# Value products in the order of head pairs 0, 2, 1, 3, and the seven-product first layer one step earlier

## The chip, the cores and the metric

The kernel runs on one core of a Trainium2 chip. A core has five engines that run side by side, each through its own queue of instructions in order: TensorE (PE, matmuls, with a weight load PEld for each), VectorE (DVE), ScalarE (ACT), GpSimd (POOL) and SyncE (SP), which here issues DMA transfers. They wait for each other through semaphores. The metric is the device time of one execution in microseconds; a profile is one execution taken by the hardware profiler, and its span runs from its first instruction to its last.

## The reference

Attention with pooled keys and values, followed by a two-layer MLP. There are 8 batches, 8 heads, 576 tokens and head size 64; the MLP has 512 inputs, 2048 hidden units and 512 outputs.

```
k_p = mean of k over 8 successive tokens            # 72 pooled keys for each head
v_p = mean of v over 8 successive tokens            # 72 pooled values
scores = q @ k_p.T / sqrt(64)
attn = exp(scores - max) / sum
x = attn @ v_p, heads side by side                  # 4608 tokens x 512
h = x @ w_in
out = gelu_tanh(h) @ w_out
```

## The kernel before, in words

The 4608 tokens go through in nine groups of 512: groups 0 to 7 are the first 512 tokens of a batch, and group R (number 8) collects the last 64 tokens of all eight batches. They run in the order 0 to 6, R, 7. Group 0 has its own opening. Every later group is a pass of the loop at the end of the kernel, counted by `n_`; "step n" below is the pass with `n_ == n`, so step 1 does the MLP of group 1, step 2 that of group 2, step 3 that of group 3.

A step does the two MLP layers of its group on TensorE and, between those matmuls, the attention of the next group, so that the next step finds its x ready. The work is not placed by a scheduler: the order on each engine is the order in which the kernel's text issues it. `at(hooks, s, f, ...)` hangs a function on a slot s, and the MLP calls the slot before its matmuls: slots 0 to 63 belong to the first layer, slots 64 to 175 to the second (112 matmuls of 128x256, one slot each). A function that is hung on a slot issues its instructions there, on whichever engine it uses, and each engine then takes them in that order.

The first layer comes in two forms. The plain form (`hidden_two`, then `hidden` for the other columns) makes 64 matmuls of 128x512. The fast form (`hidden_fast`) computes half of the layer with seven products in place of eight, in Strassen's manner: 56 matmuls of 128x256 (`product`, L465), 32 plain ones of 128x512 (L374), and on VectorE the differences of x that it needs (`x_sums`, L449) and the sums of the products (L493, L501, L504, L508), with copies on ScalarE. Between its first and second product it calls `rest()`, which is `values(g, 1)`: the second half of its own group's value products. Which form a step takes is decided by `fast = n_ >= 3`.

The second layer has seven products in every step: they run in the order 1, 2, 6, 5, 7, 3, 4 (L577), of 16 matmuls each. Four of the inputs are sums of activations made on VectorE by `g_sums` (L425 to L429). Products 1, 6, 7 and 4 accumulate one after another in the same PSUM tile `xs`; between them it is copied out by ScalarE (`x_copy`, L92), or added out by VectorE (`x_add`, L562), and the next product on it waits for that.

The attention of the next group, by the functions that the change touches:

- `load_kv` issues the loads of K and V on SP (L112 for the large parts, L107 and L105 for two half blocks); `load_q` those of q (L121).
- `pool` sums eight rows in three VectorE instructions (L149, L151, L152); its first is stage 0 and the other two are stage 1. Blocks 0 to 4 hold K and the first V rows, blocks 5 to 8 the rest of V.
- `dup_k`, `kT_tile` and `k_transpose_dma` (L165, L207) transpose the pooled keys by DMA, and `k_spread` copies them into the block form `kbd` (L92 or L94).
- `spread_v` multiplies the pooled values by a mask into the block form `vbd`, on POOL (L172); `spread_gated` is the same behind a small instruction that makes POOL wait.
- `cast_gated` casts q on POOL (L94), and `q_transpose_dma` transposes it on SP (L228).
- `scores` (L244), `exps` (ScalarE, L253), `sums` and `norm` (VectorE, L260, L269, L275; the second of the four on POOL), and `e_transpose_dma` (SP, L302) make the normalised weights, 128 tokens at a time. The buffers of `exps` are three for four parts.
- `values` (L337) multiplies the weights with `vbd`, 256 tokens at a time. For groups 1 to 7 a call makes 16 matmuls: eight with 32 rows (`SMALL`), then eight with 64 rows (`BIG`), and in each of the two passes two matmuls for each of four head pairs. A matmul uses one 32x64 or 64x64 tile of the array, given by the row where its weights start and by which half of the output's partitions it writes:

```
    BIG = [(64, 0), (0, 1), (64, 1), (0, 2), (0, 3), (64, 3), (0, 4), (64, 4)]
    SMALL = [(0, 1), (64, 1), (0, 2), (64, 2), (96, 2), (32, 3), (96, 3), (32, 4)]
                for pr in range(HP):
                    for hh in range(2):
                        r0, c = part[2 * pr + hh]
```

In this list head pairs 0 and 1 use the same two tiles, and so do pairs 2 and 3. The result is cast to bf16 by ScalarE and VectorE (L92, L94), and the first layer reads it.

Of the kernel before, what the change touches and what calls it, by code (L numbers as in the profile page):

```python
# [19 lines left out]
def kernel(  # L20
# [21 lines left out]
    nc = tc.nc  # L42
    B, H, S, D = q.shape
# [6 lines left out]
    HP = H // 2  # L50
# [39 lines left out]
    def copy(eng, out, in_):  # L90
        if eng is nc.scalar:
            eng.copy(out=out, in_=in_)  # L92
        else:
            eng.tensor_copy(out=out, in_=in_)  # L94
# [227 lines left out]
    def values(g, half, split=True):  # L322

        eT, t0 = st[g]["eT"], 256 * half
        if half == 0 or not split:
            xo = psum.tile([128, HP, 256], F32, name="xo", tag="sc", bufs=2)
            dst = [xo[:, pr, :] for pr in range(HP)]
        else:
            xo = [psum.tile([128, 2, 256], F32, name="xo", tag="mm", bufs=4) for _ in range(2)]
            dst = [xo[pr // 2][:, pr % 2, :] for pr in range(HP)]  # L330
        if g < B:
            for part, rows_ in ((SMALL, 32), (BIG, 64)):
                for pr in range(HP):
                    for hh in range(2):
                        r0, c = part[2 * pr + hh]
                        n = dict(PARTS[pr])[c]
                        nc.tensor.matmul(out=dst[pr][64 * hh:64 * hh + 64],  # L337
                                         lhsT=vbd[r0:r0 + rows_, g, n, 64 * hh:64 * hh + 64],
                                         rhs=eT[r0:r0 + rows_, 2 * half:2 * half + 2, c, :],
                                         start=(part is SMALL and pr % 2 == 0), stop=(part is BIG), skip_group_check=True)  # L340
        else:
            for pr in range(HP):
                for b in range(4):
                    p0 = 64 * (b % 2)
                    for x, (c, n) in enumerate(PARTS[pr]):
                        nc.tensor.matmul(out=dst[pr][:, 64 * b:64 * b + 64], lhsT=vbd[:, 4 * half + b, n, :],  # L346
                                         rhs=eT[:, 2 * half + b // 2, c, p0:p0 + 64], start=(x == 0), stop=(x == 1))
        xT = st[g]["xT"]
        if half == 0 or not split:
            copy([nc.scalar, nc.vector][half], xT[:, :, t0:t0 + 256], xo)  # L350
        else:
            for i, eng in enumerate((nc.scalar, nc.vector)):
                copy(eng, xT[:, 2 * i:2 * i + 2, t0:t0 + 256], xo[i])
# [408 lines left out]
    def at(hooks, s, f, *a):  # L762
        hooks.setdefault(s, []).append(lambda: f(*a))

    def tail_of_attention(hooks, n, va):
        at(hooks, va, xT_tile, n)
        at(hooks, va, nc.scalar.preload_act_table_set, GELU_SET)
        at(hooks, va, values, n, 0)
        at(hooks, va, values, n, 1, False)

    hooks = {}
# [46 lines left out]
    for n_, g in enumerate(seq):  # L818
        if n_ == 0:
            continue  # L820
        hooks = {}
        fast = n_ >= 3
        if n_ == 1:
            for i in range(1, 4):
                at(hooks, i, w_sums, i, 0, NP, nc.vector)
            at(hooks, 36, g_sums, 0, 4)
            at(hooks, 57, g_sums, 4, 6)
        elif fast:
            at(hooks, 41, g_sums, 0, 2, (0,))
            at(hooks, 57, g_sums, 2, 6, (0,))  # L830
            at(hooks, 65, g_sums, 6, 8, (0,))
            at(hooks, 65, g_sums, 0, 8, (1,))
        else:
            at(hooks, 20, g_sums, 0, 2)
            at(hooks, 36, g_sums, 2, 4)
            at(hooks, 57, g_sums, 4, 6)
        if not fast:
            at(hooks, 65, g_sums, 6, 8)
        if n_ + 1 < len(seq):
            n = seq[n_ + 1]  # L840
            b = B - 1 if n == R else n
            kv = n != B - 1
            if n_ == 1:
                for j in range(4):
                    at(hooks, 28 + 4 * j, cast_q, n, j, j + 1, nc.scalar)
                at(hooks, 41, qT_tile, n)
                at(hooks, 41, q_transpose_dma, n)
            if kv and not fast:
                t0 = 22 if n_ == 1 else 12
                at(hooks, t0, pool, b, 0, 5)  # L850
                at(hooks, t0, dup_k, b, 0, 5)
                at(hooks, t0, kT_tile, b, None)
                at(hooks, t0, k_transpose_dma, b)
                t1 = t0 + (16 if n_ == 1 else 24)
                at(hooks, t1, pool, b, 5, 9)
                at(hooks, t1, spread_v, b, nc.gpsimd)
                at(hooks, 56, k_spread, b, [nc.vector, nc.vector])
            elif kv:
                at(hooks, 17, pool, b, 0, 5, (1,))
                at(hooks, 17, dup_k, b, 0, 5)  # L860
                at(hooks, 17, kT_tile, b, None)
                at(hooks, 17, k_transpose_dma, b)
                at(hooks, 17, spread_gated, b)
                at(hooks, 40, k_spread, b, [nc.gpsimd, nc.gpsimd])
            if fast:
                at(hooks, 2, qT_tile, n)
                at(hooks, 2, q_transpose_dma, n)
                sc_at = [76, 76, 100, 100]
                norm_at = [84, 88, 106, 106]
            else:  # L870
                sc_at = [68, 68, 94, 94]
                norm_at = [81, 97, 104, 114]
            for j in range(4):
                at(hooks, sc_at[j], scores, n, j)
                at(hooks, max(sc_at[j], 80), exps, n, j)
            at(hooks, norm_at[0], eT_tile, n)
            if fast:
                for j in (2, 3):
                    at(hooks, norm_at[j], sums, n, j)
            for j in range(4):  # L880
                at(hooks, norm_at[j], norm, n, j, nc.gpsimd if j == 1 else nc.vector)
                at(hooks, norm_at[j], e_transpose_dma, n, j)
            at(hooks, 64 + 66, nc.scalar.preload_act_table_set, GELU_SET)
            at(hooks, 64 + 100, xT_tile, n)
            at(hooks, 64 + 100, values, n, 0)
            if n_ < 2:
                at(hooks, 64 + 107, values, n, 1)
        if n_ + 2 < len(seq):
            n2 = seq[n_ + 2]
            s2 = 44 if n_ == 1 else 8 if n2 == R else 57  # L890
            at(hooks, s2, q_tile, n2)
            if n2 == R:
                at(hooks, s2, load_q, n2, 0, 2, nc.sync)
                at(hooks, 30, load_q, n2, 2, 4, nc.sync)
            else:
                at(hooks, s2, load_q, n2, 0, 4, nc.sync)
            at(hooks, 64 + 52, cast_gated, n2)
            if n_ < 2:
                at(hooks, 64 + 100, qT_tile, n2)
                at(hooks, 64 + 100, q_transpose_dma, n2)  # L900
                at(hooks, 64 + 100, load_kv, n2, (1,))
            elif n2 != B - 1:
                b2 = B - 1 if n2 == R else n2
                at(hooks, 64 + 84, pool, b2, 5, 9, (0,))
                at(hooks, 64 + 97, pool, b2, 5, 9, (1,))
                at(hooks, 64 + 98, pool, b2, 0, 5, (0,))
            if n_ == 1:
                at(hooks, 45, load_kv, n2, (0,))
            else:
                at(hooks, 28, load_kv, n2)  # L910
        mlp(g, hooks, n_ + 1 == len(seq), fast, lambda: values(g, 1))
# [30 lines left out]
```

## Time and profile before

| what | us |
|---|---|
| median of 3 runs (280.68 to 280.84) | 280.75 |
| the profiled execution | 280.68 |
| its span | 278.8 |
| PE busy in it | 271.8 |
| DVE busy | 224.3 |
| ACT busy | 176.3 |
| POOL busy | 64.7 |
| value products of groups 1 to 7 (L337), one call of 16 matmuls | 0.70 |

A row of a timeline gives the start in us from the beginning of the span, the length in us, the engine, the line, the operation, what it writes and reads, the shapes and the count; in brackets stands how long the engine was idle before it and what ended that. The chain that ended last gives start, length and what ran. A row of a table by stretch gives the stretch, its length, then the busy time and the count of PE, PEld, DVE, ACT and POOL, then the granted clock, the DMA share and GB/s.

### The profile page before, as it was taken

The page shows a single profiled execution, that of the slowest core. Times are in us where ns is not written, and L with a number is a line of the kernel's source. Part 1 is how long each engine was busy: PE and PEld are TensorE (multiplying, and loading weights), DVE is VectorE, ACT ScalarE, POOL GpSimd, SP SyncE. Part 2 cuts the span into 40 slices and gives each one's busy share as a digit, 9 for nine tenths or more (in the row PEclk, how much of TensorE's full clock was granted, in tenths as well). Part 3 has the DMA queues.
Part 4 walks back from the last instruction along what each step waited for, and adds up shares of the span by engine and source line. Part 5 has one row for each costly group of instructions (what it writes and reads, how often), then busy time and mean ns, then how long its engine had stood idle before and what let it go on. Part 6 is the DMA issues. An engine that isn't in the chain of part 4 may idle for free.

```text
span 278.8 us, 6535 instructions
## 1 busy us (share of the span) xinstructions
PE 271.8 (97%) x2686; PEld 191.8 (69%) x2686; DVE 224.3 (80%) x370; ACT 176.3 (63%) x258; POOL 64.7 (23%) x103
## 2 busy tenths in 40 slices
PE   8989999999999999999999999999999999999995
PEld 3668844445864587668766876687668966876684
DVE  5886869999966989989898989898989378937832
ACT  1586575487637764796479647964796469647820
POOL 4640162003130314221422142214221300100000
PEclk9999999999999999999999999999999999999999
DMA  7999999998989895998579969996941550263013
GB/s 227 310 195 296 372 386 212 312 334 204 264 186 250 275 261 150 168 281 235 161 161 267 251 162 209 224 239 168 159 150 27 160 137 2 26 141 83 1 40 113
DMA packets 71695, 54.36 MB, mean 195 GB/s; under 512 B 45554, under 2 KB 57842, under 8 KB 71666
## 3 DMA queue, kind: packets, MB, share of 16 engines
q1 hardware_dynamic: 69410, 51.72, 72.7%
q0 software_dynamic: 2112, 2.10, 4.7%
q8 instruction: 21, 0.34, 0.5%
q10 hardware_dynamic: 144, 0.13, 0.1%
q14 instruction: 8, 0.07, 0.1%
HBM read 36.70 MB, written 9.44 MB: 165 GB/s over the span
## 4 chain that ended last, share of the span: by engine, by line
PE 87%; DVE 7%; DMA 4%; SPq 1%; issue 0%; POOL 0%
PE mm L577 33%; PE mm L374 22%; PE c L465 13%; PE mm L385 5%; PE xo L337 3%; PE x L577 3%; PE sc L244 2%; DMA q_sb<-in_q_dram 2%; DMA qT<-q_b 2%; DVE den L260 1%; PE mm L522 1%; DVE eb L275 1%; PE mm L390 1%; DVE kv L149 1%; DVE eb L287 1%; PE xo L346 1%
## 5 line engine op out<-in xcount | busy, mean ns | idle before, releaser
L374 PE MATMUL mm<-xT,w_in_b 128*128 128x512 bf16 x304 | 69.9, 379 | 0.0
L577 PEld LDWEIGHTS <-gT 128*128 128x128 bf16 x512 | 48.7, 98 | 8.9 <-issue 1.4
L376 ACT ACTIVATE gT<-mm 128x512 bf16<-128x512 f32 x76 | 43.9, 598 | 15.3 <-PE mm L374 14.9
L374 PEld LDWEIGHTS <-w_in_b 128*128 128x128 bf16 x304 | 29.7, 98 | 30.7
L577 PEld LDWEIGHTS <-stage 128*128 128x128 bf16 x384 | 37.2, 98 | 4.5
L92 ACT CAST xT<-xo 128x512 bf16<-128x512 f32 (+1 forms) x17 | 13.4, 786 | 31.1 <-PE xo L337 26.2
L172 POOL TENSOR_TENSOR vbd<-kvb,vmask 128x256 bf16<-128x256 bf16 (+2 forms) x40 | 22.2, 578 | 36.4 <-DVE kvb L152 27.4
L577 PE MATMUL mm<-tw,gT 128*128 128x256 bf16 x240 | 30.0, 273 | 0.0
L260 DVE TENSOR_REDUCE den<-e 128x8 f32<-128x576 f32 x36 | 26.1, 738 | 4.4 <-ACT e L253 4.4
L577 PE MATMUL mm<-w_out_b,gT 128*128 128x256 bf16 x240 | 29.1, 273 | 0.0
L92 ACT COPY osb<-mm 128x512 f32<-128x512 f32 x30 | 17.6, 585 | 18.0 <-PE mm L577 16.8
L577 PE MATMUL mm<-tw,stage 128*128 128x256 bf16 x224 | 27.6, 273 | 0.0
L253 ACT ACTIVATE e<-sc 128x576 f32<-128x576 f32 x36 | 22.5, 654 | 6.5 <-PE sc L244 3.9
L275 POOL TENSOR_TENSOR eb<-e,r 128x576 bf16<-128x576 f32 x7 | 8.0, 1149 | 72.3 <-DVE r L269 66.1
L94 POOL CAST q_b<-q_sb 128x1024 bf16<-128x1024 f32 (+1 forms) x15 | 19.3, 1307 | 19.1 <-DMA q_sb<-in_q_dram 19.1
L149 DVE TENSOR_TENSOR kv<-kv 128x1024 f32<-128x1024 f32 (+3 forms) x19 | 21.0, 1106 | 3.3 <-DMA kv<-in_k_dram 2.2
L465 PEld LDWEIGHTS <-ws 128*128 128x128 bf16 x192 | 18.8, 98 | 6.0
L275 DVE TENSOR_TENSOR eb<-e,r 128x576 bf16<-128x576 f32 x25 | 20.0, 799 | 0.9
L94 DVE CAST xT<-xo 128x512 bf16<-128x512 f32 (+1 forms) x10 | 7.5, 745 | 13.5 <-PE xo L337 8.3
L465 PE MATMUL c<-tt,ws 128*128 128x256 bf16 x144 | 17.7, 273 | 0.0
L425 DVE TENSOR_TENSOR stage<-gT 128x512 bf16<-128x512 bf16 (+1 forms) x25 | 13.1, 526 | 3.4 <-ACT gT L481 1.9
L385 PE MATMUL mm<-xT,w_in_b 128*128 128x256 bf16 x128 | 15.6, 273 | 0.1
(105 smaller groups left out, 413.5 us busy)
## 6 DMA issues: line engine op xcount, KB each, us to landing
kv<-in_k_dram SPq DMA_DIRECT2D x7, 1024.0 KB, 6.7
q_sb<-in_q_dram SPq DMA_DIRECT2D x7, 1024.0 KB, 9.6
kv<-in_v_dram SPq DMA_DIRECT2D x6, 1024.0 KB, 8.2
out_dram<-osb SPq DMA_DIRECT2D x12, 512.0 KB, 3.2
out_dram<-osb SPq DMA_DIRECT2D x11, 256.0 KB, 3.3
kv<-in_v_dram SPq DMA_DIRECT2D x4, 512.0 KB, 10.1
w_in_b<-in_moe_w_in_dram POOLq DMA_DIRECT2D x4, 512.0 KB, 6.7
w_out_s<-in_moe_w_out_dram SPq DMA_DIRECT2D x2, 1024.0 KB, 13.4
```

What stands on the lines that cost most here:

```text
L92: eng.copy(out=out, in_=in_)
L94: eng.tensor_copy(out=out, in_=in_)
L149: add(out=t[:, :, 0:4, :], in0=t[:, :, 0:4, :], in1=t[:, :, 4:8, :], op=ALU.add)
L172: eng.tensor_tensor(out=vbd[p0:128, b, n0:n1, :].rearrange("p (c r) (hh d) -> p c (r hh) d", c=max(m, 1), d=D), in0=kvb[p0:128, 4 + c0:4 + ...
L253: nc.scalar.activation(out=e.rearrange("p (x h) s -> p x (h s)", x=2), in_=sc[:, :, 0:4 * Sp], func=ACT.Exp, scale=1.0 / 64.0)
L260: nc.vector.reduce_sum(out=den, in_=e, axis=AX.X)
L275: eng.tensor_tensor(out=o.rearrange("p (pr hh s) -> p hh pr s", hh=2, s=Sp), in0=e.rearrange("p (hh pr) s -> p hh pr s", hh=2), in1=r.rear ...
L374: nc.tensor.matmul(out=hp, lhsT=w_in_b[:, ko, fo * 128:(fo + 1) * 128], rhs=st[g]["xT"][:, ko, :], start=(i == 0), stop=(i == KO - 1))
L376: nc.scalar.activation(out=gT[:, fo, :], in_=hp, func=ACT.Gelu_apprx_tanh)
L385: nc.tensor.matmul(out=hp[:, f, :], lhsT=w_in_b[:, ko, (fo + f) * 128:(fo + f + 1) * 128], rhs=st[g]["xT"][:, ko, c0:c0 + 256], start=(ko ...
L465: nc.tensor.matmul(out=acc[:, m, :], lhsT=lhs(i, m), rhs=rhs(i), start=bool(fresh and i == 0 and m % 2 == 0), stop=(i == 1), skip_group_ch ...
L577: nc.tensor.matmul(out=xs[p] if acc is xs else acc[:, p, :], lhsT=lt, rhs=rt, start=bool(fresh and m == 0 and (p == 0 or (last and acc is ...
```

## The change

The value products of groups 1 to 7 go through the head pairs in the order 0, 2, 1, 3, so that four successive matmuls are given four different tiles of the array.

Step 2 takes the fast form of the first layer (`fast = n_ >= 2`). With it, the second half of group 2's value products is made by `rest()` inside step 2, no longer at slot 171 of step 1. The rest of step 2's schedule becomes that of the fast steps: the sums of activations at their slots, the scores at 76 and 100, the norms at 84 to 106, `k_spread` on POOL at slot 40, the transposes of q at slot 2 (it was slot 164 of step 1). The first pooling stage of group 3's K runs at slot 162 of step 1, and its second stage at slot 17 of step 2. The load of group 3's V moves from slot 164 of step 1 to slot 3 of step 2, behind the transpose of q. Its pooling, all three instructions, and its spread stand at slot 41 of step 2 (in steps 3 and later, the pooling of V is done at slots 148 and 161 of the step before, and the spread at slot 17).

```diff
--- before.py
+++ after.py
@@ -330,7 +330,7 @@
             for part, rows_ in ((SMALL, 32), (BIG, 64)):
-                for pr in range(HP):
+                for pr in (0, 2, 1, 3):
                     for hh in range(2):
@@ -819,7 +819,7 @@
-        fast = n_ >= 3
+        fast = n_ >= 2
@@ -860,11 +860,17 @@
                 at(hooks, 17, k_transpose_dma, b)
-                at(hooks, 17, spread_gated, b)
+                if n_ == 2:
+                    at(hooks, 41, pool, b, 5, 9)
+                    at(hooks, 41, spread_v, b, nc.gpsimd)
+                else:
+                    at(hooks, 17, spread_gated, b)
                 at(hooks, 40, k_spread, b, [nc.gpsimd, nc.gpsimd])
             if fast:
                 at(hooks, 2, qT_tile, n)
                 at(hooks, 2, q_transpose_dma, n)
+                if n_ == 2:
+                    at(hooks, 3, load_kv, n, (1,))
                 sc_at = [76, 76, 100, 100]
                 norm_at = [84, 88, 106, 106]
@@ -883,8 +889,6 @@
             at(hooks, 64 + 100, values, n, 0)
-            if n_ < 2:
-                at(hooks, 64 + 107, values, n, 1)
@@ -895,14 +899,11 @@
             at(hooks, 64 + 52, cast_gated, n2)
-            if n_ < 2:
-                at(hooks, 64 + 100, qT_tile, n2)
-                at(hooks, 64 + 100, q_transpose_dma, n2)
-                at(hooks, 64 + 100, load_kv, n2, (1,))
-            elif n2 != B - 1:
+            if n2 != B - 1:
                 b2 = B - 1 if n2 == R else n2
-                at(hooks, 64 + 84, pool, b2, 5, 9, (0,))
-                at(hooks, 64 + 97, pool, b2, 5, 9, (1,))
+                if n_ >= 2:
+                    at(hooks, 64 + 84, pool, b2, 5, 9, (0,))
+                    at(hooks, 64 + 97, pool, b2, 5, 9, (1,))
                 at(hooks, 64 + 98, pool, b2, 0, 5, (0,))
```

## The prediction

> **What bounds the kernel now.** I read the page's busy times and the chain that ended last, then the same chain in order of time, then busy times per step, then single instructions of VectorE and TensorE.
>
> ```profile
> PE 271.8 (97%) x2686; PEld 191.8 (69%) x2686; DVE 224.3 (80%) x370; ACT 176.3 (63%) x258; POOL 64.7 (23%) x103
> PE 87%; DVE 7%; DMA 4%; SPq 1%; issue 0%; POOL 0%
> ```
>
> TensorE sets the end, but VectorE's 80% is an average. In order of time, the first value products of steps 1, 2 and 3 and the scores of step 2 stand in the chain like this:
>
> ```profile
> 78.77 0.70 PE xo L337 x16
> ...
> 96.10 0.38 PE sc L244 x32
> ...
> 99.43 0.57 PE sc L244 x32
> ...
> 107.75 0.70 PE xo L337 x16
> ...
> 135.58 0.70 PE xo L337 x16
> ```
>
> So step 2, which has the plain first product, takes 107.75 - 78.77 = 28.98 us, and step 3, which has the seven-product form, 27.83 us. Busy times in these two stretches:
>
> ```profile
> 78.77:107.75 28.98, 28.97 (x276) 18.25 (x280) 22.67 (x42) 18.34 (x28) 6.27 (x10) 1.00 0.99 240
> 107.75:135.58 27.83, 27.83 (x300) 20.49 (x304) 25.59 (x42) 19.04 (x26) 8.12 (x13) 1.00 0.81 208
> ```
>
> TensorE (first pair after the length) is never idle in either. VectorE (third) has 2.2 us free in step 3: this is what the change must live on. Step 3 is my template: the changed step 2 has its instructions, with one block more on VectorE. A time t of step 3 is t - 28.98 in step 2. VectorE's rows of step 3 around that place, and the TensorE product that waits for the last of them:
>
> ```profile
> 121.51 0.43 DVE L427 TENSOR_TENSOR stage<-gT 128x512 bf16<-128x512 bf16 x1
> 122.27 0.69 DVE L425 TENSOR_TENSOR stage<-gT 128x1024 bf16<-128x1024 bf16 x1 [0.33 <-ACT gT L481]
> 127.18 0.75 DVE L260 TENSOR_REDUCE den<-e 128x8 f32<-128x576 f32 x1 [0.19 <-ACT e L253]
> 133.50 0.69 DVE L562 TENSOR_TENSOR osb<-mm,osb 128x512 f32<-128x512 f32 x1
> 134.98 0.60 PE L577 MATMUL mm<-tw,gT 128*128 128x256 bf16 x4
> ```
>
> From 121.94 to 134.19 VectorE pauses only 0.33 and 0.19 us. L562 reads the PSUM pieces xs, into which product 4 accumulates next, from 134.98: the margin is 134.98 - 134.19 = 0.79 us.
>
> **The fast form itself.** Removed are 64 matmuls of 128x512 (1.89 + 12.09 = 13.98 us in the chain); added are 56 of 128x256 and 32 of 128x512, which in step 3 take 0.87 + 0.98 + 1.73 + 1.75 + 0.86 + 0.87 + 0.86 + 1.75 + 3.45 = 13.12. The second scores go from 0.57 to 0.38, since they come later than the exponentials that free their PSUM. With small shifts the whole is the difference of the steps: -1.15 us. The form's sums and copies on VectorE and ScalarE are in the template.
>
> **The block that step 3 does not have.** Group 3's value rows are pooled wholly at hook 41 of step 2 (three VectorE instructions), just after the 121.51 row, where step 3 has none. Their price, and what POOL does meanwhile, stand in steps 1 and 2:
>
> ```profile
> 90.69 1.22 DVE L149 TENSOR_TENSOR kv<-kv 128x1024 f32<-128x1024 f32 x1
> 91.94 0.69 DVE L151 TENSOR_TENSOR kv<-kv 128x512 f32<-128x512 f32 x1
> 92.67 0.43 DVE L152 TENSOR_TENSOR kvb<-kv 128x256 bf16<-128x256 f32 x1
> 93.01 0.93 DVE L94 COPY kbd<-kTd 64x288 bf16<-64x288 bf16 x2
> ...
> 65.35 1.90 POOL L172 TENSOR_TENSOR vbd<-kvb,vmask 128x256 bf16<-128x256 bf16 x3
> 65.52 0.73 DVE L425 TENSOR_TENSOR stage<-gT 128x512 bf16<-128x512 bf16 x1
> 66.35 0.65 DVE L426 TENSOR_TENSOR gT<-gT 128x512 bf16<-128x512 bf16 x1
> 67.91 0.42 DVE L425 TENSOR_TENSOR stage<-gT 128x512 bf16<-128x512 bf16 x1
> 68.44 0.42 DVE L426 TENSOR_TENSOR gT<-gT 128x512 bf16<-128x512 bf16 x1
> ```
>
> The three take 93.01 - 90.69 = 2.32 us, start to start. They release POOL's four spreads (2.47 us in steps 1 and 2), which then run beside the next VectorE sums of gT, L425 and L426, at 128x1024. Beside spreads these sums were slower at 128x512: 0.73 against 0.42 and 0.65 against 0.42, factors 1.74 and 1.55. On 0.69 each that is 0.51 + 0.38 = 0.9 us. Bounds: nothing, if the longer form doesn't suffer (L149 took 1.22 at 134.11 beside POOL's casts and 1.22 at 90.69 with POOL idle), and the spreads' own 2.47 if it were held off altogether. I take 0.9, from the same instructions.
>
> So VectorE is later at L562 by 2.32 - 0.33 - 0.19 + 0.9 = 2.70 us, and product 4 starts 2.70 - 0.79 = 1.91 us late: +1.91. Two earlier waits lie inside this. Product 7 must wait for ScalarE's copy of xs (L92, 129.94 in step 3), queued behind the fourth exponential, which waits for VectorE's first norm to free its buffer. Product 6 needs the last L427 (125.73, so 128.6 now) for its seventh matmul at about 128.7. Transposes of eb are late too, but TensorE is then as late; the last landed 0.57 us before use in step 3 (138.00 against 138.57), so up to 0.3 may be added.
>
> The Trainium skill's "SBUF — State Buffer", section "SBUF: two separate sides", says that VectorE with two SBUF inputs and GpSimd exclude each other for a whole instruction, the loser being fully blocked. The rows above show slowing by half to three quarters, not a stop; by the rule taken fully the 0.9 would be 2.47 and the result 282.9.
>
> **The V load.** Group 3's V (1 MB, L112) goes on SP from right behind a transpose in step 1 (issued 82.89) to behind step 1's second output store and the qT transpose, which itself moves from 79.56 to about 110.96 - 28.98 = 81.98. This transpose held SP 4.23 us in step 3 and 3.26 in step 4, so V is issued between 85.3 and 86.2. Landing took 7.3 us for this V, 6.2 for the K load behind step 4's transpose, 8.2 as the median of V loads: landed between 91.5 and 94.4. VectorE asks for it at 121.94 - 28.98 = 92.96. I take no wait (nearest: 6.2 to 7.3, most below 93); the upper end is 1.5 us, added one for one, because VectorE is in order and everything above is queued behind it. The kT transpose (L207, about 87.5) now follows V; landing took 2.6 in step 3 and 8.1 in step 2, then 0.9 for POOL's two copies into kbd: 91.0 to 96.5, wanted by the scores at 96.0. I take nothing; at worst 0.5. qT lands by 88.8, 7 us early.
>
> **Moved at no cost.** The first pooling pass of group 3's K (1.48 us) goes to the end of step 1, into the 2.06 us in which VectorE waits for the value products before its xT cast; without that gap it would delay the cast by as much. kbd's copies leave VectorE for POOL (0.9 us, POOL idle there). The second half's value products go behind the first product of step 2, as in the template.
>
> **The value order.** Each set of 16 takes 0.70 us, 14 sets (x224). In the written order the third matmul needs the same tile as the first. Yet this is a set seen up to 135.515 and up to 135.530:
>
> ```profile
> 135.51 0.29 PE L337 MATMUL xo<-eT,vbd 32*64 32x256 bf16 x2
> ...
> 135.51 0.31 PE L337 MATMUL xo<-eT,vbd 32*64 32x256 bf16 x4
> ```
>
> Four have started, and none of the next four follows up to 135.640: four tiles already work at once. The scores, written in four-tile order, have four started within some 10 ns of the first, the value products within some 16. So the new order can win about 8 ns for each of two passes per set (an estimate from these starts): 14 x 16 ns = -0.2 us. Bounds: zero, and one round of about 0.13 us in each pass if order counted, 14 x 0.26 = -3.7.
>
> The Trainium skill, "TensorE: Matmul & The Clock Gate", section "The mechanism", has matmuls start and end strictly in program order; by that the new order saves the whole round, and the time would be some 277.7. The four early starts speak against it.
>
> **Sum.** The profiled execution took 280.68 us (span 278.8 and 1.9 around it), 0.07 below the median of 280.75. -1.15 + 1.91 - 0.2 = +0.56: 281.24 on its own scale, 281.3 on the median's. I put 281.4, leaning to the side of the unpriced waits (V, last eb transpose).
>
> **Rivals.** (1) Sums unhurt by POOL: stall 1.01, -1.15 + 1.01 - 0.2 = -0.34: 280.4. For it: only 128x512 is measured. (2) V late by up to 1.5: 282.0 to 282.8. (3) Faster: VectorE's delay never reaches product 4, so that TensorE keeps all: -1.15 - 0.2, 279.4. It decides at 0.79 + 0.52 = 1.31 us of extra VectorE work; the block is 2.32 bare, so pooling would have to shrink or pauses that I don't see absorb it. (4) The order works as written: -3.7 on top, about 277.6.
>
> **How the numbers follow.** Chances: main case 0.45 (280.8 to 281.8 by itself), (1) 0.17, (2) 0.22, (3) 0.12, (4) 0.04. 0.2% is 0.56 us, about what a measurement tells from no change. The main case's centre lies at that bound, so it is split, a little more going to slower; slower is 0.28 of it with (2), 0.50; same is (1) with the remaining 0.17, 0.34; faster is (3) and (4), 0.16. The range drops (4), most of (3) and the far end of (2): 279.7 to 282.7.
>
> **What would show it.** Right: after the block, L425 and L426 at 128x1024 over 1 us; a TensorE gap of about 1.9 us in step 2's output product, released by VectorE's L562 (or L92 on ScalarE before product 7); step 2 about 29.7 us, other steps as before; value sets 0.68 to 0.70. Wrong: no such gap, VectorE idle in front of L149 on in_v, or value sets near 0.45.

## The result

The changed kernel takes 282.00 us (median of 4 runs, 281.58 to 282.34) against 280.73 (280.68 to 280.84) for the kernel before on the same chip: ratio 1.0044, 95% interval 1.0027 to 1.0061. It is slower by 1.27 us. The predicted time was 281.4, its range 279.7 to 282.7, and slower had the largest chance, 0.50.

The profiled execution took 282.34 us with a span of 280.6, so it is the longest of the four. Against the one of before (280.68) it is 1.66 longer.

### The profile after

The page's busy times and the shares of the chain that ended last:

```profile
PE 271.6 (97%) x2710; PEld 193.7 (69%) x2710; DVE 228.5 (81%) x370; ACT 176.9 (63%) x256; POOL 66.9 (24%) x105
...
PE 79%; DVE 15%; DMA 3%; issue 1%; ACT 0%; POOL 0%; DVEq 0%; ACTq 0%; POOLq 0%
```

TensorE is as busy as before, but VectorE's part of the chain went from 7% to 15%. Steps 2, 3 and 4, by the starts of their first value products (stretch, length, busy time and count of PE, PEld, DVE, ACT and POOL, clock, DMA share, GB/s):

```profile
78.93:109.06 30.13, 28.21 (x296) 20.33 (x296) 26.76 (x41) 18.83 (x26) 7.52 (x12) 1.00 0.81 229
109.06:137.38 28.32, 28.12 (x301) 20.57 (x304) 26.14 (x42) 19.14 (x26) 8.65 (x13) 1.00 0.83 206
137.38:165.19 27.81, 27.81 (x300) 20.50 (x304) 25.32 (x41) 19.03 (x26) 7.84 (x13) 1.00 0.82 214
```

TensorE, never idle in these steps before, is idle for 30.13 - 28.21 = 1.92 us in step 2 and 0.20 in step 3. The stretches are cut by the rows of the chain; taken from first matmul to first matmul, as in all that follows, the steps are:

| kernel | step 1 | 2 | 3 | 4 | 5 | 6 | 7 |
|---|---|---|---|---|---|---|---|
| before | 29.79 | 28.98 | 27.83 | 27.83 | 27.83 | 27.74 | 28.19 |
| after | 29.93 | 30.22 | 28.23 | 27.81 | 27.81 | 27.71 | 28.19 |

So +0.14, +1.24, +0.40 and, by the unrounded starts, -0.08 for the other four; opening and tail make +0.16. Together this is 1.86 us, the difference of the two spans (280.63 against 278.78). The 0.14 and 0.16 are no more than such parts differ between executions: in the runs below that keep step 1 of the kernel after, it lay between 29.45 and 30.03, the opening between 48.79 and 49.26. The rows of TensorE that begin after a wait (how long it was idle and what ended that stands in the brackets):

```profile
100.42 1.26 PE L577 MATMUL mm<-tw,stage 128*128 128x256 bf16 x10 [0.45 <-DVE stage L427]
...
104.60 1.91 PE L577 MATMUL mm<-tw,stage 128*128 128x256 bf16 x16 [1.17 <-ACT osb L92]
...
108.55 0.60 PE L577 MATMUL mm<-tw,gT 128*128 128x256 bf16 x4 [0.29 <-DVE osb L562]
...
120.99 1.03 PE L465 MATMUL c<-tt,w_in_b 128*128 128x256 bf16 x8 [0.20 <-DVE stage L504]
```

The first three are in step 2's output products, ahead of the seventh matmul of product 6, of product 7 and of product 4, as expected. The last is in step 3. VectorE in step 2, from the block on:

```profile
93.31 1.42 DVE L149 TENSOR_TENSOR kv<-kv 128x1024 f32<-128x1024 f32 x1
...
95.84 0.68 DVE L425 TENSOR_TENSOR stage<-gT 128x1024 bf16<-128x1024 bf16 x1
96.56 1.03 DVE L426 TENSOR_TENSOR gT<-gT 128x1024 bf16<-128x1024 bf16 x1
97.62 0.98 DVE L427 TENSOR_TENSOR stage<-gT 128x1024 bf16<-128x1024 bf16 x1
98.53 0.83 DVE L425 TENSOR_TENSOR stage<-gT 128x512 bf16<-128x512 bf16 x1
...
107.81 0.68 DVE L562 TENSOR_TENSOR osb<-mm,osb 128x512 f32<-128x512 f32 x1
```

L149 starts as soon as the L427 before it ends: V had landed at 91.48, so nothing waits for the load. L425 starts 2.53 us after L149, and of the sums L426, L427 and the next L425 are slow (0.69, 0.69 and 0.42 undisturbed). POOL's spreads, in its own rows, run beside these three:

```profile
96.43 3.19 POOL L172 TENSOR_TENSOR vbd<-kvb,vmask 128x256 bf16<-128x256 bf16 x4 [2.78 <-DVE kvb L152]
```

In step 3 the chain that ended last runs through a store (start, length, what):

```profile
109.62 0.61 DVE osb L599
...
110.25 3.63 DMA out_dram<-osb
...
113.96 1.02 ACT osb L491
...
120.99 1.03 PE c L465 x8
```

VectorE, late from step 2, finishes L599 late; the output store goes out late; ScalarE's L491, which overwrites that buffer with the first product of step 3, waits for it (its own cast before it was done at 113.41 or so); and so down to TensorE.

### The profile page after: what moved, and what is told of

It reads as the page before. It is cut to its first block, busy times and chain, and to the rows that moved or that the text cites. A ratio compares the mean times of both kernels' runs of the same rounds, so it can differ in the third digit from the quotient of the medians.

```text
span 280.6 us, 6585 instructions
## 1 busy us (share of the span) xinstructions
PE 271.6 (97%) x2710; PEld 193.7 (69%) x2710; DVE 228.5 (81%) x370; ACT 176.9 (63%) x256; POOL 66.9 (24%) x105
## 4 chain that ended last, share of the span: by engine, by line
PE 79%; DVE 15%; DMA 3%; issue 1%; ACT 0%; POOL 0%; DVEq 0%; ACTq 0%; POOLq 0%
PE mm L577 28%; PE mm L374 18%; PE c L465 13%; PE mm L385 5%; PE xo L337 3%; PE x L577 2%; DVE den L260 2%; PE warm L676 2%; DVE eb L275 2%; PE sc L244 2%; DVE kv L149 2%; DMA qT<-q_b 2%; DMA out_dram<-osb 1%; PE mm L390 1%; DVE kv L151 1%
## 5 line engine op out<-in xcount | busy, mean ns | idle before, releaser
L374 PE MATMUL mm<-xT,w_in_b 128*128 128x512 bf16 x280 | 65.2, 379 | 0.0
L577 PEld LDWEIGHTS <-gT 128*128 128x128 bf16 x512 | 48.9, 98 | 9.2 <-issue 1.7
L376 ACT ACTIVATE gT<-mm 128x512 bf16<-128x512 f32 x70 | 40.1, 598 | 12.7 <-PE mm L374 12.4
L374 PEld LDWEIGHTS <-w_in_b 128*128 128x128 bf16 x280 | 27.4, 98 | 27.1
L577 PEld LDWEIGHTS <-stage 128*128 128x128 bf16 x384 | 37.0, 98 | 6.5 <-issue 1.3
L577 PE MATMUL mm<-tw,gT 128*128 128x256 bf16 x240 | 29.9, 273 | 0.3 <-DVE osb L562 0.3
L577 PE MATMUL mm<-tw,stage 128*128 128x256 bf16 x224 | 28.0, 273 | 1.6 <-ACT osb L92 1.2
L577 PE MATMUL mm<-w_out_b,gT 128*128 128x256 bf16 x240 | 28.9, 273 | 0.0
L172 POOL TENSOR_TENSOR vbd<-kvb,vmask 128x256 bf16<-128x256 bf16 (+2 forms) x40 | 22.9, 596 | 25.1 <-DVE kvb L152 24.2
L465 PEld LDWEIGHTS <-ws 128*128 128x128 bf16 x224 | 21.9, 98 | 7.2 <-issue 0.2
L149 DVE TENSOR_TENSOR kv<-kv 128x1024 f32<-128x1024 f32 (+3 forms) x19 | 21.2, 1117 | 3.6 <-DMA kv<-in_k_dram 2.4
L465 PE MATMUL c<-tt,ws 128*128 128x256 bf16 x168 | 20.8, 273 | 0.0
L465 PEld LDWEIGHTS <-w_in_b 128*128 128x128 bf16 x168 | 15.9, 98 | 3.3 <-issue 1.6
```

The costliest lines, as they stand in the source:

```text
L149: add(out=t[:, :, 0:4, :], in0=t[:, :, 0:4, :], in1=t[:, :, 4:8, :], op=ALU.add)
L172: eng.tensor_tensor(out=vbd[p0:128, b, n0:n1, :].rearrange("p (c r) (hh d) -> p c (r hh) d", c=max(m, 1), d=D), in0=kvb[p0:128, 4 + c0:4 + ...
L374: nc.tensor.matmul(out=hp, lhsT=w_in_b[:, ko, fo * 128:(fo + 1) * 128], rhs=st[g]["xT"][:, ko, :], start=(i == 0), stop=(i == KO - 1))
L376: nc.scalar.activation(out=gT[:, fo, :], in_=hp, func=ACT.Gelu_apprx_tanh)
L465: nc.tensor.matmul(out=acc[:, m, :], lhsT=lhs(i, m), rhs=rhs(i), start=bool(fresh and i == 0 and m % 2 == 0), stop=(i == 1), skip_group_ch ...
L577: nc.tensor.matmul(out=xs[p] if acc is xs else acc[:, p, :], lhsT=lt, rhs=rt, start=bool(fresh and m == 0 and (p == 0 or (last and acc is ...
```

## The experiments

The theory: the value order is worth nearly nothing, the fast form wins 1.15 us in step 2, and the pooling block at slot 41, with POOL's spreads beside the sums behind it, costs more than that, through VectorE's L562. The rivals: the order does matter, or V is late, or the loss lies in the fast form itself and not in the block.

### The order of the value products

The kernel before, with the new order alone:

```diff
-                for pr in range(HP):
+                for pr in (0, 2, 1, 3):
```

> The kernel before with nothing changed but the order of the head pairs (0, 2, 1, 3). Theory (four tiles work at once already, whatever the order): a set of 16 goes from 0.70 to 0.68 us, 14 sets, so -0.2 to -0.35 us on 280.73. Rival (matmuls start in program order): one round less in each pass, about -3.7 us, 277.0. Rival (the new order itself is what costs time): slower than 280.73 by some of the 1.3 us.

281.10 us (12 runs) against 281.03 (30): ratio 1.0007, interval 0.9995 to 1.0018. In the chain that ended last a set of 16 went from 0.70 to 0.68 in step 2's row and 0.69 in step 3's. Steps 3 to 5 are 27.81 or 27.82 in place of 27.83: by the unrounded starts the order is worth 0.01 to 0.03 us a step, too little for the time to show. The opposite order, in which each matmul is followed by one on its own tile (A A B B C C D D), makes the case sharper (again in the kernel before):

```diff
-                for pr in range(HP):
-                    for hh in range(2):
+                for hh in range(2):
+                    for pr in range(HP):
```

> The kernel before; the two loops of the value products exchanged, so that in program order every tile is used by two successive matmuls (A A B B C C D D). Theory (a matmul whose tile is free starts ahead of an earlier one whose tile is busy): a set stays at 0.70 us within 0.04, the time within 0.4 us of 280.73. Rival (program order): five rounds for each pass, where the same rule needs three for the order of before: 28 passes with two rounds of about 0.11 to 0.13 us more, 286.9 to 288.0.

281.25 us, ratio 1.0007 (0.9996 to 1.0018). The row of step 2's last set in that chain:

```profile
107.70 0.70 PE xo L337 x16
```

Still 0.70. If each matmul waited for the one before it on its tile and kept the next ones waiting, this order would have lengthened the set well past the 0.70 of the written one. Matmuls on free tiles therefore do not queue behind one whose tile is taken, at least over the distance of this list. The starts in the trace fit this. The first four matmuls of a set begin at 0, 3, 7 and 10 ns in the new order (A B C D), at 0, 4, 14 and 17 in the written one (A B A B C D C D) and at 0, 7, 13 and 20 in this one; the fifth follows at about 134 in all three. That is some 3.3 ns for each place in the list, and a matmul whose tile is taken costs the next ones its place and no more. The rule of the Trainium skill, "TensorE: Matmul & The Clock Gate", section "The mechanism", that matmuls stay in program order, does not hold for the starts of such small tiles here.

The rest of the change alone, that is, the kernel after in the old order:

```diff
-                for pr in (0, 2, 1, 3):
+                for pr in range(HP):
```

> The changed kernel with the old order of the head pairs: the fast step 2 alone. Theory: the changed kernel's 282.0 plus the 0.2 to 0.35 us of the order, 282.2 to 282.4, with the same TensorE waits in step 2 (L427, L92, L562, together 2.4 us by the starts of the products). Rival (the order costs): less than 282.0.

282.07 us, ratio 1.0047 (1.0031 to 1.0064); TensorE's waits in step 2 are again 1.2, 0.3 and 0.3 us, on the same three lines; step 2 takes 30.13 us and step 3 28.53. The whole loss is the fast step's.

### The block and the spreads

One of the three pooling instructions is kept, so that the block is 0.6 us in place of 2.3. The two first additions of group 3's V pooling are left out, so this kernel does less than the reference asks for:

```diff
+    def pool_last(b, c0, c1):
+        t = st[b]["kv"][:, c0:c1]
+        nc.vector.tensor_tensor(out=st[b]["kvb"][:, c0:c1, 0, :], in0=t[:, :, 0, :], in1=t[:, :, 1, :], op=ALU.add)
...
-                    at(hooks, 41, pool, b, 5, 9)
+                    at(hooks, 41, pool_last, b, 5, 9)
```

> The changed kernel; of the pooling of group 3's V at slot 41 of step 2 only the last of three VectorE instructions is left (the two additions before it are left out, so group 3's values are sums of two rows instead of eight). Loads, spread and order stay. Theory (the block delays VectorE and TensorE waits at product 4): VectorE is some 2.1 us earlier behind the block, its delay at L562 falls from 3.1 to about 1.0 us against a margin of 0.73, TensorE loses 0.3 instead of 2.4 us in step 2 and nothing in step 3: 279.3 to 279.9. Rival (the fast form costs this by itself: its stores, PSUM or copies): stays above 281.3.

280.36 us, ratio 0.9979 (0.9967 to 0.9991): faster than the kernel before, by less than expected. Step 2 is 28.21, step 3 28.47. TensorE's product 4 in step 2 (lines are 4 higher in this kernel, L566 is L562), POOL's spreads, and ScalarE in step 3:

```profile
106.37 0.60 PE L581 MATMUL mm<-tw,gT 128*128 128x256 bf16 x4 [0.25 <-DVE osb L566]
...
93.73 4.17 POOL L176 TENSOR_TENSOR vbd<-kvb,vmask 64x128 bf16<-64x128 bf16 x5
...
111.89 1.01 ACT L495 COPY osb<-c 128x1024 f32<-128x1024 f32 x1 [0.65 <-DMA out_dram<-osb]
```

The block's length is the cause of most of the loss: 28.21 against 30.22. What was missed are two things that the shorter block doesn't take away: the five spreads now lie beside the sums in one piece of 4.17 us and slow six of them, and step 3 waits for its store here too.

Next, the block stays whole and the spreads go behind POOL's norm, away from the sums:

```diff
-                    at(hooks, 41, spread_v, b, nc.gpsimd)
+                    at(hooks, 89, spread_v, b, nc.gpsimd)
```

> The changed kernel; group 3's spread on POOL stands behind POOL's own norm (slot 89) instead of at slot 41, so that it runs beside the norms and no longer beside VectorE's sums of gT. The pooling block stays. Theory (POOL's spreads slow the bf16 sums by about 1.05 us): L425 to L427 behind the block at 0.69 and 0.42 again, the delay at L562 from 3.1 to 2.1 to 2.4 us, TensorE loses 1.4 to 1.7 us in step 2 instead of 2.4; ratio to the kernel before from 1.0044 to 1.0010 to 1.0025. Rival (the sums are slow for another reason): the sums stay at 0.8 to 1.0 and the ratio at 1.004.

281.77 us, ratio 1.0037 (1.0023 to 1.0051), above what was expected. A row of it on VectorE, and TensorE's value products at the start of step 3:

```profile
96.03 0.69 DVE L426 TENSOR_TENSOR gT<-gT 128x1024 bf16<-128x1024 bf16 x1
...
108.87 0.63 PE L337 MATMUL xo<-eT,vbd 32*64 32x256 bf16 x9 [0.82 <-POOL vbd L172]
```

The first part came out as priced: without the spreads beside them the sums are 0.68 and 0.69 us again, and step 2 is 29.14, that is 1.08 less. But the spreads, at 104.42 and 4.39 us long, now end after the value products want them (0.82), and the store is late again (ScalarE's L491 waits 1.01 for it): step 3 takes 29.81. What step 2 won, step 3 gave back, and by the time this kernel can't be told from the kernel after (1.0044).

To be rid of that, the spreads were held by a one-element copy that reads the last sum, and so run between the sums and POOL's norm:

```diff
+    def spread_late(b):
+        nc.gpsimd.tensor_copy(out=gate, in_=sums_[:, 2, 7, 255:256])
+        spread_v(b, nc.gpsimd)
...
-                    at(hooks, 41, spread_v, b, nc.gpsimd)
+                    at(hooks, 66, spread_late, b)
```

> The changed kernel with group 3's four spreads held by a one-element copy on POOL that reads the last sum's result, so that they start only when VectorE's sums of gT are done (about 101.6) and end before POOL's norm at 104.3; the block on VectorE stays at slot 41. Theory (the spreads cost the sums 1.05 us, and nothing else that they touch is urgent there): sums at 0.68 and 0.42, step 2 29.1 us as with the spread behind POOL's norm, and, other than there, no late values: step 3 28.2 as in the changed kernel. Ratio 1.0005 to 1.0020. Rival (VectorE's reductions and norms suffer beside the spreads as the sums did, 1 us in another place): step 2 29.9 to 30.3, ratio 1.0035 to 1.0050.

281.65 us, ratio 1.0038 (1.0026 to 1.0051): by the time, the rival's numbers; by the profiled execution, which was this kernel's fastest (281.39), in between, with step 2 at 29.54 and step 3 at 28.03. The sums are 0.68 to 0.69 and no value product waits. What remains of TensorE's waits is 0.50 us ahead of product 7 and 0.91 ahead of product 4 (L582 is L577 and L567 is L562):

```profile
PE mm L582 <- DVE osb L567: 0.9, 1, 0.9
```

The 0.91 was 0.45 in the run before, and step 2 is 0.4 longer than expected: the spreads take 3.12 us here, so that POOL's norm stands 0.4 us later in the step (103.95 to 105.1), and the VectorE norm beside it took 1.37 us, where it takes 0.76 with POOL idle. It is POOL's norm that slows it, and not the spreads: the VectorE norm at 101.25, which runs beside them, took its usual 0.76.

Twice the spreads at slot 41, the other way round:

```diff
                     at(hooks, 41, spread_v, b, nc.gpsimd)
+                    at(hooks, 41, spread_v, b, nc.gpsimd)
```

> The changed kernel with group 3's spread made twice in a row on POOL at slot 41 (some 3 us more of POOL, which is free until its norm). Theory (VectorE's bf16 sums are slowed while POOL spreads): the 128x512 sums and L429 behind the block are slowed too, 0.4 to 1.0 us more delay at L562 and as much on TensorE; ratio 1.006 to 1.008. Rival (only the block's own length counts): unchanged, 1.004.

282.48 us, ratio 1.0062 (1.0045 to 1.0079), step 2 at 30.45: the ratio is at the lower end of what was expected, and its interval overlaps that of the kernel after, so the rows must tell. Five more spreads are worth 0.23 us in the step, where 0.4 to 1.0 was expected: they slow the last sums alone (L427 at 128x512 took 0.51, L429 1.52, where 0.42 and 1.22 are usual).

Then the block itself goes to POOL, with the spreads behind POOL's norm once more. VectorE's sums should then run nearly free, if the two engines only slow each other a little:

```diff
-    def pool(b, c0, c1, stages=(0, 1)):
+    def pool(b, c0, c1, stages=(0, 1), eng=nc.vector):
...
-        add = nc.vector.tensor_tensor
+        add = eng.tensor_tensor
...
-                    at(hooks, 41, pool, b, 5, 9)
-                    at(hooks, 41, spread_v, b, nc.gpsimd)
+                    at(hooks, 41, pool, b, 5, 9, (0, 1), nc.gpsimd)
+                    at(hooks, 89, spread_v, b, nc.gpsimd)
```

> The changed kernel; the three additions that pool group 3's V run on POOL instead of VectorE, and the spread stands behind POOL's norm. Theory (the block on VectorE is what TensorE waits for): VectorE has no block; POOL's additions, about 3.5 us by the rate of its norm (1.15 us for 576 fp32), slow the sums beside them by 0.3 to 0.4 us for each us: delay at L562 about 1.0 to 1.5 us, TensorE loses 0.3 to 0.8 us in step 2 and up to 0.6 in step 3; ratio 0.997 to 1.000. Rival (VectorE and POOL hold each other off for whole instructions): POOL's additions cost VectorE as much as its own did, ratio 1.003 or more.

283.11 us, ratio 1.0080 (1.0061 to 1.0098): the slowest of all, and the rival's case. Step 2 takes 30.64 us, against 29.14 with the block on VectorE and the spreads in the same place. The first of its rows on POOL and the sum beside it on VectorE:

```profile
93.82 2.76 POOL L149 TENSOR_TENSOR kv<-kv 128x1024 f32<-128x1024 f32 x1
...
94.40 2.72 DVE L426 TENSOR_TENSOR gT<-gT 128x1024 bf16<-128x1024 bf16 x1
```

L426 takes 0.69 us by itself. Here it ends 0.54 after POOL's first addition ends (97.12 against 96.58), L427, 1.64 long, 0.55 after the second (98.80 against 98.25), the next L425, 0.95 long, 0.28 after the third: each waits out nearly the whole of one POOL instruction and then does its own work. That is the rule of the Trainium skill's "SBUF — State Buffer", section "SBUF: two separate sides", and not the mere slowing that the prediction read from its rows. On this reading the two engines take turns when the spreads are of some 0.6 us each, and a sum loses at most what is left of one spread (0.29 to 0.41 us in the kernel after); beside an addition of 2.76 us it loses nearly all of that.

### The late store in step 3

In the kernel after, L149 of group 4's V stands ahead of L599 on VectorE, and the store waits for L599. The addition is moved behind it, in step 2 only:

```diff
-                    at(hooks, 64 + 84, pool, b2, 5, 9, (0,))
+                    at(hooks, 64 + (97 if n_ == 2 else 84), pool, b2, 5, 9, (0,))
```

> The changed kernel; at the end of step 2 the first pooling addition of group 4's V (L149, 1.22 us) stands behind VectorE's last sum of the output (L599) instead of ahead of it, so that the first output store is issued 1.1 us earlier. Theory (what step 3 loses, 0.5 us, is ScalarE's L491 waiting for that store to free its buffer): L491 follows its xT cast at once, step 3 back to 27.8 us, step 2 unchanged; ratio from 1.0044 to 1.0025 to 1.0030. Rival (step 3 is late because VectorE is behind with its casts): step 3 stays at 28.3.

282.97 us, ratio 1.0077 (1.0061 to 1.0094): slower, where a gain was expected. Step 2 is the same 30.22, step 3 28.63. The chain of step 3:

```profile
109.70 4.81 DMA out_dram<-osb
...
114.59 1.02 ACT osb L491
```

L599 was done at 109.33, 0.9 us earlier, but SP was then busy with the transposes of eT until 109.6, and the store took 4.81 us to land in place of 3.63. So what L491 waits for is when the store lands, and that is not set by VectorE alone. The single packets in the trace tell what else sets it. The store goes as 128 packets of 4 KB and ends in 16 short writes, one, as I read it, for each of the 16 DMA engines. Fifteen of these came by 112.17, the last at 114.02; in the kernel after, fifteen by 112.53 and the last at 113.39. In both runs a 16 KB packet of the queue that brings instructions lies in this stretch, from 110.69 to 112.39 here and from 110.52 to 111.76 there, and the late part of the store begins just as it ends (112.38 and 111.75). The trace doesn't name the engine of a packet, so that both were on the same one is inferred from these times.

So the late store of the kernel after has two causes. VectorE's lateness brings it into the instruction packet, and the packet costs it some 0.9 us (an estimate, from 113.39 and 112.53); without this it would have landed at about 113.0, before ScalarE's own cast was done at 113.41. Issued 0.55 us earlier, it met the same packet, which was longer in this run. In the kernel before, the instruction packet of this stretch starts at 111.53 and falls on the second store of the pair, for which TensorE doesn't wait.

### Can the block go elsewhere?

If the block is all that costs, the fast step should win once the block stands where VectorE is idle: 2.04 us ahead of the xT cast at the end of step 1. For that V must be loaded in step 1 with K, and q, to make room, later.

```diff
+                if n_ == 1:
+                    at(hooks, 64 + 99, pool, b2, 5, 9)
...
-                at(hooks, 45, load_kv, n2, (0,))
+                at(hooks, 45, load_kv, n2)
...
-            s2 = 44 if n_ == 1 else 8 if n2 == R else 57
+            s2 = 160 if n_ == 1 else 8 if n2 == R else 57
...
-            at(hooks, 64 + 52, cast_gated, n2)
+            at(hooks, 161 if n_ == 1 else 64 + 52, cast_gated, n2)
...
-                if n_ == 2:
-                    at(hooks, 41, pool, b, 5, 9)
-                    at(hooks, 41, spread_v, b, nc.gpsimd)
-                else:
-                    at(hooks, 17, spread_gated, b)
+                at(hooks, 17, spread_gated, b)
...
-                if n_ == 2:
-                    at(hooks, 3, load_kv, n, (1,))
```

> The changed kernel without its block in the middle of step 2: group 3's V is loaded together with its K in step 1 (slot 45), its three pooling instructions stand at slot 163 of step 1, in the 2.04 us in which VectorE waits for the value products, and its spread is the gated one of the later steps (slot 17 of step 2). To make room among the transfers, group 3's q is loaded at slot 160 of step 1 and cast at slot 161. Nothing is left out. Theory (all that is lost comes from the block at slot 41, by its own length, the spreads beside the sums behind it, and the late store): step 2 becomes the template, 27.8 to 28.0 us, step 3 27.8; the xT cast behind the block in step 1 is 0.3 late at most. The whole: -1.15, some -0.1 for the value order, +0 to 0.3: ratio 0.9955 to 0.9975. Rival (the fast form itself costs as much as it saves, wherever the block is, because the stages of step 2 depend on loads, transposes and VectorE's order of a later step): step 2 at 28.6 or more, ratio 0.999 or more.

281.82 us, ratio 1.0034 (1.0016 to 1.0052), step 2 at 30.43: the rival's numbers, but through a store, which the rival did not name. The three waits in the output products are gone, and in their place stands one in the first layer:

```profile
89.79 1.03 PE L465 MATMUL c<-tt,ws 128*128 128x256 bf16 x8 [1.92 <-DVE stage L501]
...
88.73 1.01 ACT L498 COPY osb<-c 128x1024 f32<-128x1024 f32 x1 [2.83 <-DMA out_dram<-osb]
```

The row names VectorE's L501, which ended within 0.06 us of ScalarE's L498; both empty a PSUM tile. L498 was 2.5 us late, because step 1's second store stood behind the q load on SP and landed at 88.63 in place of 84.70; L501 was 1.1 late, the last 0.8 of it in L165 beside POOL's cast of q. So q was put behind that store, at the start of step 2:

```diff
+                if n_ == 2:
+                    at(hooks, 1, q_tile, n)
+                    at(hooks, 1, load_q, n, 0, 4, nc.sync)
+                    at(hooks, 1, cast_gated, n)
...
-                at(hooks, 2, q_transpose_dma, n)
+                at(hooks, 18 if n_ == 2 else 2, q_transpose_dma, n)
...
```

> The kernel with the early block, once more, with its q load out of the way of the stores: group 3's q is loaded and cast at slot 1 of step 2, behind both output stores of step 1, and transposed at slot 18, behind the transpose of kT. In the run before, the q load stood ahead of the second store, which landed at 88.63 in place of 84.70; ScalarE's copy L498, which overwrites that buffer, began at 88.73 in place of 86.24, and TensorE waited 1.92 us for the PSUM tile that it empties. Nothing is left out. Theory (that store was the whole reason): L498 near 86.3, no TensorE gap in the first layer of step 2, the step 27.8 to 28.5 (the upper end if the transposes of eT, behind the later loads of group 4, land after their use: they made 0.48 in the run before), ratio 0.9955 to 0.9985. Rival (with the block in step 1 something else of the early schedule is late, such as qT or kT at the scores, so that the fast form wins nothing there either): step 2 above 28.9, ratio 0.9995 or more.

282.11 us, ratio 1.0046 (1.0017 to 1.0075). L498 starts at 86.29 and TensorE runs without a pause from there to the value products at the end of step 2, which it reaches at 106.78. Then:

```profile
109.17 0.75 PE L337 MATMUL xo<-eT,vbd 32*64 32x256 bf16 x16 [2.39 <-DMA eT<-eb]
```

The whole saving and more is lost in one wait (step 2 takes 30.27): the transposes of eT were issued from 100.78 on, behind group 4's loads, which began 3.6 us later than in the kernel after (92.47 against 88.88) and whose last, q, landed at 107.32. The last version spreads these loads as well: q of groups 4 to 6 (and half of R's) at the start of the step that uses it, half of the next K in the pause while q is cast.

```diff
+                at(hooks, 17, kv_tile, b2)
+                at(hooks, 17, load_main, b2, "k", 0, 2, nc.sync)
+                at(hooks, 28, load_main, b2, "k", 2, 4, nc.sync)
...
-                if n_ == 2:
+                late = n_ <= 6
+                if late:
...
-                    at(hooks, 1, load_q, n, 0, 4, nc.sync)
+                    at(hooks, 1, load_q, n, 2 if n == R else 0, 4, nc.sync)
...
```

> The kernel with the early block and the late q, with the later loads spread to match: in steps 2 to 5 the next group's q is loaded and cast at slot 1 of its own step (as group 3's in the run before) and transposed behind kT; half of the K load of the group after it goes at slot 17, ahead of that transpose, and the rest of K and V at slot 28; group R's q goes half at slot 30 of step 5, half at slot 1 of step 6. Nothing is left out. In the run before, TensorE won the whole saving up to the value products and then waited 2.39 us for the transposes of eT, which landed behind group 4's q load (107.32). Theory (the bytes loaded between 82 and 107 were the whole reason: 4.2 MB, of which 1 MB now goes a step later and 0.5 MB into a pause of the queues): K and V of group 4 land by 103, eT in time, step 2 at 27.8 to 28.2, the later steps 27.8 with perhaps 0 to 1.5 once in step 5; ratio 0.994 to 0.999. Rival (the eT transposes land late in every step that loads q at its start, because all these transfers come later than in the kernel before): several steps above 28.2, ratio 1.000 or more.

282.68 us, ratio 1.0070 (1.0046 to 1.0094). Its profiled execution was its fastest (281.43). Step 2 there, in the table by stretch:

```profile
78.87:106.68 27.81, 27.71 (x296) 20.47 (x297) 26.57 (x41) 18.97 (x26) 8.15 (x12) 1.00 0.78 210
```

K and V of group 4 landed by 102.94 here and the transposes of eT in time, so those loads were the reason in the run before. Step 2 takes 27.81 us, 1.17 less than before: the fast form wins in step 2 what was priced, when its block is out of the way. But steps 3, 5 and 6, at 28.25, 28.49 and 28.08, are 0.42, 0.66 and 0.34 longer than before (a wait for L504, one for the transposes of eT, one for L504 again), step 1 0.31 and the tail 0.56. The other five executions were 0.4 to 2.8 us longer than this one, and of these there is no trace, so where they lose is open. No version tried beats the kernel before with all of its work done.

## Why the prediction was right

**The fast form, -1.15.** Right: step 2 was 1.17 shorter in the last experiment, where the block stood outside it (some 0.03 of this is the value order).

**The value order, -0.2.** Its sign was right, its size at most that: 0.01 to 0.03 us a step in the order-only run, 0.68 for a set in place of 0.70 against an estimate of 0.016 each for 14 sets. The fourth rival (order as written, -3.7) is out.

**The V load, no wait.** Right: landed 91.48, asked for at 93.31. With it the second rival is out, though the time came out at the lower end of its range.

**The block, 2.32.** Right in place and nearly in size: 2.53 us from 93.31 to 95.84, since the first spread already met L149 (1.42 in place of 1.22).

**POOL beside the sums, 0.9.** The step whose size was off. The working took only L425 and L426 at 128x1024. POOL's copies of kT met the first sums too (+0.19), the first spread met L149 (+0.21), and the others, which took 3.19 us and not 2.47, met L426, L427 and the next L425 (+0.63 and +0.42): 1.45 in all, with a lower and an upper bound of 0 and 2.47 on record. The first rival (sums unhurt) is out, by the rows and by the run with the late spreads, which took back 1.08. The reading behind it, that such rows show "slowing by half to three quarters, not a stop", was wrong: beside long POOL instructions each sum waits for nearly a whole one. The other price on record, the spreads' whole 2.47, was too high: beside the short spreads and copies VectorE lost 1.45 in all.

**Pauses and margin, 0.33 + 0.19 and 0.79.** Right: 0.33 and 0.27 were absorbed. L562 was then 3.13 us late in place of 2.70, and product 4 by 2.39 = 3.13 - 0.79 + 0.05. The idle rows sum to 1.91, by chance the predicted number: a row's idle time starts at the modelled end of the matmul before it (0.27 us long, while one follows another every 0.109), so each of the three gaps costs 0.16 more than it shows.

**Not priced: step 3.** +0.40, through the store that L599 releases and the instruction packet that this store then meets. The prediction followed VectorE's lateness to TensorE's next wait, and left it there; but it also holds the store, and that buffer's next writer is a step away. The question that it asked of each stall, what is late next, was not asked of this one, and its sign "other steps as before" did not hold.

Step 2 so came out at -1.15 + 2.39 = +1.24 where +0.76 was put, and step 3 adds 0.40. That is why the time is 0.6 above the central number, and above the 280.8 to 281.8 that the main case was given by itself. That it still lies in the stated range is luck: the range was kept open upwards for a late V load, which did not come.

**The third rival**, faster at less than 1.31 us of extra VectorE work, has some support: with a block of about 0.6 us, in a kernel that leaves work out, the time was 0.67 us shorter than before, where 1.35 was put. The difference is again in the spreads, which with what is left of the block cost step 2 0.4 us there, and in the store in step 3.

## What to carry to other kernels

A step that takes over a faster form must be priced with all that the form's place in the schedule lacks: here one pooling block, which cost twice what the form wins, because the engine that took it was in order and the critical one waited on its last result. When such a block is moved away, follow the bytes and the stores as well as the engines: each of three moves freed TensorE in one place and let a transfer be late in another. And a rate of slowing that is read from short instructions side by side does not hold for long ones.

## What the runs showed of the hardware

- Small matmuls on different tiles of the array need no order in the program: A B A B, A B C D and A A B B gave 0.70, 0.68 and 0.70 us for a set of 16. The first four start within 20 ns in each order.
- An addition of two SBUF operands on VectorE and one on POOL exclude each other for a whole instruction: 0.69 us became 2.72 beside one of 2.76. Not every pair of two-operand instructions shows it: VectorE's norm took its usual 0.76 us beside the spreads (in the runs with doubled and with held spreads) and 1.37 beside POOL's norm. POOL pays as well: the five spreads took 2.59 us in the first kernel with the early block and 4.39 in the one with them behind POOL's norm, beside VectorE's norms, L562 and L149.
- The three additions of V's pooling took 2.76, 1.60 and 1.06 us on POOL against 1.22, 0.69 and 0.42 on VectorE, with VectorE's sums in their way.
- A store of 512 KB took 2.7 to 9.1 us from issue to landing, by what was queued on the DMA engines ahead of it: 7.0 behind the 1 MB load of q in the first kernel with the early block, 9.1 behind that of V, and a transpose, in the order-only run.
- Such a store lands with the last of its sixteen parts, and one 16 KB instruction packet was enough to hold that part back, by some 0.9 us in the kernel after and 1.85 in the run in which the addition stands behind L599.
